# Zero writes to the row memory and the scatters in front of them, declared independent

## The chip, the cores and the metric

The kernel runs on one core of one Trainium2 chip. The metric is the device time of one execution in microseconds (us), as the median of several runs; the kernel before has a median of 2022.66 us over 3 runs (2016.06 to 2024.6).

## The reference

A causal seven-tap convolution over the sequence, per head with softmaxed weights, is followed by a mixture of eight experts, of which each token takes the best two.

```python
w = softmax(weight)                                  # 8 heads x 7 taps
out = np.einsum('hk,bskhg->bshg', w, x_unf)          # 28672 tokens x 192
noisy = x @ w_gate + log1p(exp(x @ w_noise)) * noise # 28672 x 8
top2 = the two best experts of a token, top2_w their softmax
for e in range(8):
    h = np.maximum(x[mask] @ w1[e], 0.0)             # 192 -> 1024
    out[mask] += top2_w[mask, k, None] * (h @ w2[e]) # 1024 -> 192
```

## The kernel before

The 28672 tokens go through in 28 **units** of 1024 (128 partitions by 8). A unit is convolved (VectorE, at first TensorE), scaled, and split into high and low 16-bit halves in one of two row buffers `rb` (lines 595 to 605; unit u takes buffer u % 2). Its gate values are computed from the transposed rows `xT` (eight transposing loads of the SP queue from line 636, then TensorE at line 651), and VectorE works out for each token its place in the lists of its two experts (`idx`, line 762). GpSimd (POOL) then writes the rows there: 16 indirect DMAs of 128 rows a unit, the **scatters** of line 783, into the DRAM tensor `xs`, the row memory, in which each expert has its region. The first ScalarE copy into `rb` for unit u (line 599) cannot start before the scatters of unit u - 2 have landed, since they read that buffer.

The experts work in 232 **blocks** (29 rounds by 8 experts, 256 rows each but for the first round). A block's rows come from `xs` by two transposing loads (lines 938 and 941) into one of three buffers `bT`; TensorE makes the first product into `ph` (line 858), ScalarE and VectorE turn it into `h` (lines 881, 885), TensorE makes the second product into `py` (line 895), ScalarE scales it into one of six buffers `y` (line 902), and POOL adds `y` into the output by an indirect DMA (line 907), two a block. The adds of a block wait until those of the block before have landed. A round's table of tokens and gates, `mt`, is loaded at line 803.

The lists are full up to a bound that the draw decides, so the last rows of each expert's fixed blocks may never be written. For them `zero_rows` (line 455) writes zeros: eight DMAs of 384 rows by 800 bytes on the SP queue, one for each expert, spawned when unit 6 comes to its gating (line 617). `lo_row` is 6912, the first row of that stretch in a region of 7296. `reach[u + 1]` is the highest row that the scatters of unit u can reach: at most 6144 up to unit 5, and 7168 or more from unit 6 on. The scatters from unit 6 on are made to wait for all zero writes (lines 791 to 793).

The order of the instructions on every engine is fixed at build time by a planner with estimated durations (class `Plan`); a queue does nothing out of turn. Waits are put in by the tile framework from what the instructions read and write. Since an indirect DMA may write anywhere in `xs`, the framework sees each scatter and each zero write as writes to the same memory and orders them, unless they are declared independent (`tc.declare_no_dep` with a group's name).

Of the kernel before, what the change touches and what calls it, by code (L numbers as in the profile page):

```python
# [9 lines left out]
F16 = mybir.dt.float16  # L10
# [8 lines left out]
P = 128  # L19
TU = 8  # L20
ROW = 400
# [111 lines left out]
def kernel(  # L133
# [11 lines left out]
    nc = tc.nc  # L145
# [51 lines left out]
    zero = const.tile([P, ROWF], F32, name="zero")  # L197
# [59 lines left out]
    init = []  # L257
    lo_row = max(0, min(cap - P, int(mean * U - 3.3 * sigma * math.sqrt(U)) // P * P))
    reach = [0]
# [8 lines left out]
    def mark(*key):  # L268
        return marks.setdefault(key, Mark())

    def done(*key, after=0.0):
        plan.mark(mark(*key), after)
# [164 lines left out]
    scat, zeroed = {}, []  # L437
# [17 lines left out]
    def zero_rows():  # L455
        nz = (cap - lo_row) // P
        for e in range(E):
            yield SP, 0.5
            init.append(nc.sync.dma_start(
                xs[e * REG + lo_row:e * REG + cap, :].rearrange("(p r) c -> p r c", p=P),  # L460
                zero.bitcast(F16)[:, None, :].to_broadcast([P, nz, ROW])))
        done("zero rows")

    def loads_first():
# [76 lines left out]
    def due(u):  # L541
        n, t = at_block
        return t + sum(EACH * rounds[i // E][1] / BIG for i in range(n, needed[min(u, U - 1)] * E))
# [64 lines left out]
    def gating():  # L608
        for u in range(U):
# [7 lines left out]
            if u == 6:  # L617
                plan.spawn(zero_rows())
# [144 lines left out]
            scat[u] = []  # L763
            done("routed", u)
            plan.spawn(scatters(u, rbf, idx), 0.3)

    def needs(a, b):
        tc.add_manual_dep(a.ins, b.ins.name, mybir.DependencyInfo(
            mybir.DependencyClass.Sync, mybir.DependencyReason.DATA), reason="data in DRAM")

    def apart():
        nc.gpsimd.nop()

    def scatters(u, rbf, idx):
        if u:
            yield mark("scattered", u - 1)
        if reach[u + 1] > lo_row:
            yield mark("zero rows")
        for i in range(2 * TU):
            t, k = i // 2, i % 2  # L780
            yield POOL, 1.4
            apart()
            s = nc.gpsimd.indirect_dma_start(  # L783
                out=xsf, out_offset=bass.IndirectOffsetOnAxis(ap=idx[:, k, t:t + 1], axis=0),
                in_=rbf[:, t, :], in_offset=None)
            for v in scat:
                tc.declare_no_dep(s.ins, group=f"scat{v}", reason="every routed row has its own place")
            tc.declare_no_dep(s.ins, group="loads", reason="rows behind those of the blocks done")
            scat[u].append(s)
            tc.add_to_no_dep_group(f"scat{u}", s.ins)  # L790
            if reach[u + 1] > lo_row:
                for z in init:
                    needs(s, z)
            slack = (due(u) - 45.0 - plan.now) / (2 * TU - i)
            if u > 1:
                yield plan.now + min(2.6, max(0.0, slack - 1.4))
        done("scattered", u, after=2.5)
# [364 lines left out]
```

## Time and profile before

| what | value |
|---|---|
| median of the runs | 2022.66 us |
| the profiled execution, its own time | 2030.29 us |
| its span | 2028.3 us |
| TensorE busy | 1946.0 us, 96% |
| VectorE, POOL, ScalarE busy | 1557.7, 1263.0, 804.2 us |
| mean granted TensorE clock | 0.986 of full speed |

The page's engine lines say who is busy; the views of waits and the timelines say for what the others wait. POOL's busy time leaves out about 0.3 us of issue ahead of each of its 904 indirect DMAs.

### The profile page before, as it was taken

What the parts mean: (1) busy time and instruction counts of PE and PEld (TensorE: products, weight loads), DVE (VectorE), ACT (ScalarE), POOL (GpSimd) and SP (SyncE); (2) the same over time, 40 slices, a digit from 0 to 9 for tenths busy, and PEclk for the clock granted to TensorE, in tenths of its full rate; (3) what the DMA queues carried; (4) which work ended last, traced back from release to release, by engine and by line L of the source; (5) the groups of instructions that cost most, each with busy time, mean ns of one, the idle gap of its engine ahead of it and who ended that gap; (6) DMA issues with size and microseconds to landing.
All of it is one profiled execution on the core that took longest, in us unless ns stands there. A gap on an engine that the chain in (4) does not pass through costs nothing. (4 is left out here: it accounts for less than half of the span.)

```text
span 2028.3 us, 52446 instructions
## 1 busy us (share of the span) xinstructions
PE 1946.0 (96%) x21703; PEld 1785.3 (88%) x21703; DVE 1557.7 (77%) x4042; ACT 804.2 (40%) x1173; POOL 1263.0 (62%) x915
## 2 busy tenths in 40 slices
PE   7779999999999999999999999999989999999997
PEld 7668899898999999989989888899989999999996
DVE  7799899898998989989888887788778865333332
ACT  4464444333444444334433333334333333333332
POOL 0566776577666767676666667666666666633333
PEclk9889999999999999999999999999999999999999
DMA  8845566877787767677766676667766765444442
GB/s 242 220 101 102 111 130 116 151 134 117 130 138 133 121 116 140 117 134 127 133 122 111 113 131 124 115 112 125 115 115 96 115 113 91 85 59 64 58 58 37
DMA packets 521882, 236.99 MB, mean 117 GB/s; under 512 B 401304, under 2 KB 508824, under 8 KB 521505
## 3 DMA queue, kind: packets, MB, share of 16 engines
q1 hardware_dynamic: 433824, 142.72, 34.2%
q0 software_dynamic: 87200, 90.80, 30.0%
q8 instruction: 171, 2.80, 0.6%
q14 instruction: 79, 0.65, 0.1%
q10 hardware_dynamic: 608, 0.02, 0.0%
HBM read 40.12 MB, written 115.38 MB: 77 GB/s over the span
## 5 line engine op out<-in xcount | busy, mean ns | idle before, releaser
L907 POOL DMA_INDIRECT out_dram<-y,ids x456 | 762.8, 1673 | 534.5 <-ACT y L902 160.7
L858 PE MATMUL ph<-bT,w1s 128*128 128x256 f16 (+2 forms) x9280 | 994.3, 271 | 15.9 <-DMA bT<-xs 7.7
L895 PE MATMUL py<-w2s,h 128*128 128x192 f16 x10944 | 986.2, 247 | 22.4 <-ACT y L902 22.3
L895 PEld LDWEIGHTS <-h 128*128 128x128 f16 x10944 | 910.3, 98 | 61.1 <-issue 53.5
L858 PEld LDWEIGHTS <-w1s 128*128 128x128 f16 (+1 forms) x9280 | 786.5, 97 | 131.5 <-issue 40.3
L885 DVE SCALAR_TENSOR_TENSOR h<-ph,h 128x1024 f16<-128x1024 f32 (+1 forms) x464 | 557.8, 1202 | 340.1 <-ACT h L881 336.7
L881 ACT ACTIVATE h<-ph 128x1024 f16<-128x1024 f32 (+1 forms) x464 | 468.2, 1009 | 593.9 <-PE ph L858 577.5
L783 POOL DMA_INDIRECT xs<-rb,idx x448 | 498.5, 1113 | 212.3 <-issue 133.0
L576 DVE SCALAR_TENSOR_TENSOR xc<-xt,wt,xc 128x192 f32<-128x192 f32 x1224 | 420.3, 409 | 2.1 <-DMA xt<-zero 2.1
L902 ACT ACTIVATE y<-py,ga 128x192 f32<-128x192 f32 x456 | 191.8, 421 | 487.7 <-PE py L895 483.1
L528 PE MATMUL ph<-xt,dg 128*128 128x192 f32 x280 | 50.4, 339 | 13.9 <-DMA xt<-in_x_dram 11.7
L603 DVE TENSOR_TENSOR rb<-xc,rb 128x1024 f16<-128x1024 f32 x28 | 34.2, 1220 | 37.8 <-ACT rb L599 34.9
L528 PEld LDWEIGHTS ph<-xt,dg 128*128 128x128 f32 x280 | 47.4, 198 | 14.3 <-DVE dg L508 11.7
L599 ACT ACTIVATE rb<-xc 128x1024 f16<-128x1024 f32 x28 | 29.5, 1055 | 65.2 <-DMA xs<-rb,idx 35.2
L574 DVE TENSOR_SCALAR xc<-xt,wt 128x192 f32<-128x192 f32 x204 | 53.9, 328 | 1.3 <-DMA xt<-in_x_dram 0.7
L589 DVE TENSOR_REDUCE am<-xc 128x8 f32<-128x1536 f32 x28 | 48.9, 1748 | 4.2 <-ACT xc L583 3.7
L593 DVE TENSOR_TENSOR xc<-xc,xs 128x1536 f32<-128x1536 f32 x28 | 49.0, 1751 | 0.0
L687 DVE SCALAR_TENSOR_TENSOR t<-t,t 128x64 f32<-128x64 f32 x168 | 37.8, 225 | 5.3
L497 ACT ACTIVATE xt<-xt 128x1152 f32<-128x1152 f32 x27 | 31.2, 1154 | 0.0
L733 DVE TENSOR_REDUCE sums<-M 128x72 f16<-128x576 f16 x23 | 26.7, 1160 | 0.0
L651 PE MATMUL misc<-gparts,xT 128*128 128x32 f16 (+1 forms) x752 | 23.3, 174 | 1.4 <-DMA xT<-rb 1.4
L651 PEld LDWEIGHTS <-xT 128*128 128x128 f16 x752 | 22.7, 96 | 1.9 <-DMA xT<-rb 1.5
(142 smaller groups left out, 613.9 us busy)
## 6 DMA issues: line engine op xcount, KB each, us to landing
out_dram<-zero SPq DMA_DIRECT2D x28, 768.0 KB
xt<-in_x_dram SPq DMA_DIRECT2D x27, 768.0 KB
bT<-xs SPq DMA_TRANSPOSE x464
out_dram<-y,ids POOLq DMA_INDIRECT x456
xs<-rb,idx POOLq DMA_INDIRECT x448
w2s<-in_moe_w_dram SPq DMA_DIRECT2D x16, 384.0 KB
w1s<-in_moe_w_dram SPq DMA_DIRECT2D x8, 512.0 KB
w1s<-in_moe_w_dram SPq DMA_DIRECT2D x16, 256.0 KB
```

The source lines that it names most:

```text
L528: nc.tensor.matmul(c[:, h - h0, :TU * G].rearrange("p (t g) -> p t g", g=G), diag[h, k], xts[u][:, k:k + TU, h * G:(h + 1) * G], start=(k ...
L574: V.tensor_scalar(dst, src, wt[:, h, k:k + 1], None, op0=OP.mult)
L576: V.scalar_tensor_tensor(dst, src, wt[:, h, k:k + 1], dst, op0=OP.mult, op1=OP.add)
L589: V.tensor_reduce(am, xc, axis=AX.X, op=OP.max, apply_absolute_value=True)
L593: V.tensor_tensor(xc, xc, xsc[:, :, None].to_broadcast([P, TU, D]), op=OP.mult)
L783: s = nc.gpsimd.indirect_dma_start(out=xsf, out_offset=bass.IndirectOffsetOnAxis(ap=idx[:, k, t:t + 1], axis=0), in_=rbf[:, t, :], in_offs ...
L858: nc.tensor.matmul(ph[:, f, :T], w, x, start=opens and f // 2 not in banks[:i], stop=closes and f // 2 not in banks[i + 1:], skip_group_ch ...
L881: nc.scalar.activation(h[:, 0, half * nf:(half + 1) * nf, :T], ph[:, :, :T], AF.Relu)
L885: V.scalar_tensor_tensor(h[:, 1, hs, :T], ph[:, :, :T], 0.0, h[:, 0, hs, :T], op0=OP.max, op1=OP.subtract)
L895: nc.tensor.matmul(py[:, half, :D], h[:, a, f, ts], w2_part(e, lo, f), start=(n == 0), stop=(n == 3 * FC - 1), skip_group_check=True)
L902: nc.scalar.activation(y, py, AF.Copy, scale=gate)
L907: a = nc.gpsimd.indirect_dma_start(out=out, out_offset=bass.IndirectOffsetOnAxis(ap=ids, axis=0), in_=y, in_offset=None, compute_op=OP.add)
```

## The change

The zero writes get the group name "zero rows", and are declared independent of the scatters of the units that are already recorded and whose rows end at or below `lo_row`. The scatters of such units that are recorded after a zero write are declared independent of the group. The waits of the scatters from unit 6 on, which do reach these rows, stay.

```diff
-            init.append(nc.sync.dma_start(
+            z = nc.sync.dma_start(
                 xs[e * REG + lo_row:e * REG + cap, :].rearrange("(p r) c -> p r c", p=P),
-                zero.bitcast(F16)[:, None, :].to_broadcast([P, nz, ROW])))
+                zero.bitcast(F16)[:, None, :].to_broadcast([P, nz, ROW]))
+            for v in scat:
+                if reach[v + 1] <= lo_row:
+                    tc.declare_no_dep(z.ins, group=f"scat{v}", reason="the unit's rows lie in front")
+            tc.add_to_no_dep_group("zero rows", z.ins)
+            init.append(z)
...
             if reach[u + 1] > lo_row:
                 for z in init:
                     needs(s, z)
+            else:
+                tc.declare_no_dep(s.ins, group="zero rows", reason="rows in front of these")
```

No instruction changes its place on any engine; only waits differ. On the SP queue, among the transposes of unit 6 (`xT`) and the loads of blocks (`bT`), the two single waits for POOL's DMAs shown here go, and a third ahead of the first zero write ten rows earlier. DMASW are the semaphores of POOL's DMAs, DMAHW those of the SP queue's. Before:

```order
L636 DMA_TRANSPOSE xT<-rb_189 128x3x128 [waits DMAHW7_49]
L459 DMA xs<-zero 384x1x400 [waits DMAHW0_49,DMASW2_49]
L459 DMA xs<-zero 384x1x400 [waits DMAHW1_49]
L459 DMA xs<-zero 384x1x400 [waits DMAHW2_49]
L938 DMA_TRANSPOSE bT<-xs 128x3x256 [waits DMAHW3_49,PE_49]
L941 DMA_TRANSPOSE bT<-xs 128x256 [waits DMAHW4_49]
L459 DMA xs<-zero 384x1x400 [waits DMAHW5_49,DMASW3_49]
```

And with the change:

```order
L641 DMA_TRANSPOSE xT<-rb_189 128x3x128 [waits DMAHW7_49]
L459 DMA xs<-zero 384x1x400 [waits DMAHW0_49]
L459 DMA xs<-zero 384x1x400 [waits DMAHW1_49]
L459 DMA xs<-zero 384x1x400 [waits DMAHW2_49]
L945 DMA_TRANSPOSE bT<-xs 128x3x256 [waits DMAHW3_49,PE_49]
L948 DMA_TRANSPOSE bT<-xs 128x256 [waits DMAHW4_49]
L459 DMA xs<-zero 384x1x400 [waits DMAHW5_49]
```

What moved: nothing but the waits DMASW2 and DMASW3.

On POOL, in the scatters of unit 5 (`rb_191`) between adds of expert blocks, three scatters wait for zero writes; two of them stand here. Before:

```order
L783 DMA xs<-rb_191,idx 287744x200 [waits DMAHW1_49,DMAHW2_49,DMAHW0_49,DMASW3_49]
L907 DMA out_dram<-y,ids 28928x192 [waits DMASW7_49,DMAHW7_49,DMASW1_49,Activation_49]
L907 DMA out_dram<-y,ids 28928x192 [waits DMASW5_49,Activation_49]
L783 DMA xs<-rb_191,idx 287744x200 [waits DMAHW6_49,DMAHW5_49,DMAHW7_49,DMAHW0_49,DMASW6_49]
L783 DMA xs<-rb_191,idx 287744x200
```

And with the change:

```order
L788 DMA xs<-rb_191,idx 287744x200 [waits DMASW3_49]
L914 DMA out_dram<-y,ids 28928x192 [waits DMASW7_49,DMAHW7_49,DMASW1_49,Activation_49]
L914 DMA out_dram<-y,ids 28928x192 [waits DMASW5_49,Activation_49]
L788 DMA xs<-rb_191,idx 287744x200 [waits DMASW6_49]
L788 DMA xs<-rb_191,idx 287744x200
```

What moved: the waits for the zero writes leave unit 5. They come back in one place, the first scatter of unit 6 (`rb_189`), eleven rows on, which before waited for VectorE's `idx` alone and now waits for it and for seven DMAHW semaphores; the load of a round's table `mt` behind the zero writes names two more DMASW semaphores.

## Rows read from the trace of the kernel before

**Rows 1.** The page's first lines: span; busy us, share, instructions by engine.

```profile
span 2028.3 us, 52446 instructions
PE 1946.0 (96%) x21703; PEld 1785.3 (88%) x21703; DVE 1557.7 (77%) x4042; ACT 804.2 (40%) x1173; POOL 1263.0 (62%) x915
```

**Rows 2.** Waits, 340 to 420 us, POOL and SP: us in total, times, longest.

```profile
POOL xs L783 <- DMA xs<-zero: 15.7, 3, 7.8
SPq L459 <- DMA xs<-rb,idx: 10.2, 3, 3.9
```

**Rows 3.** POOL's timeline: start, duration, instruction, [idle before, releaser].

```profile
343.16 2.02 POOL L907 DMA_INDIRECT out_dram<-y,ids  x1 [0.30 <-issue]
...
357.60 0.98 POOL L783 DMA_INDIRECT xs<-rb,idx  x1 [2.13 <-DMA xs<-zero]
...
378.87 1.00 POOL L783 DMA_INDIRECT xs<-rb,idx  x1 [7.80 <-DMA xs<-zero]
...
389.44 0.99 POOL L783 DMA_INDIRECT xs<-rb,idx  x1 [5.80 <-DMA xs<-zero]
...
458.60 1.98 POOL L907 DMA_INDIRECT out_dram<-y,ids  x1 [0.31 <-issue]
...
519.78 2.68 POOL L907 DMA_INDIRECT out_dram<-y,ids  x1 [0.30 <-issue]
526.50 1.56 POOL L907 DMA_INDIRECT out_dram<-y,ids  x1 [4.04 <-ACT y L902]
...
1044.69 1.59 POOL L907 DMA_INDIRECT out_dram<-y,ids  x1 [0.31 <-issue]
```

**Rows 4.** ScalarE's timeline: result copies `y` and row copies `rb`.

```profile
341.74 0.42 ACT L902 ACTIVATE y<-py,ga 128x192 f32<-128x192 f32 x1 [0.96 <-PE py L895]
...
402.44 1.06 ACT L599 ACTIVATE rb<-xc 128x1024 f16<-128x1024 f32 x1 [3.51 <-DMA xs<-rb,idx]
...
439.19 0.42 ACT L902 ACTIVATE y<-py,ga 128x192 f32<-128x192 f32 x1 [1.50 <-PE py L895]
...
465.86 1.06 ACT L599 ACTIVATE rb<-xc 128x1024 f16<-128x1024 f32 x1 [6.40 <-DMA bT<-xs]
...
1031.59 0.42 ACT L902 ACTIVATE y<-py,ga 128x192 f32<-128x192 f32 x1 [1.40 <-issue]
...
1052.14 1.06 ACT L599 ACTIVATE rb<-xc 128x1024 f16<-128x1024 f32 x1 [4.30 <-DMA xs<-rb,idx]
```

**Rows 5.** TensorE's timeline: the gaps of 340 to 480 us and normal rows.

```profile
373.15 0.24 PE L651 MATMUL misc<-gparts,xT 128*128 128x32 f16 x3 [1.37 <-DMA xT<-rb]
...
403.86 2.14 PE L895 MATMUL py<-w2s,h 128*128 128x192 f16 x24 [1.72 <-ACT y L902]
...
463.15 1.91 PE L858 MATMUL ph<-bT,w1s 128*128 128x256 f16 x16
468.70 3.39 PE L895 MATMUL py<-w2s,h 128*128 128x192 f16 x24 [3.65 <-ACT y L902]
471.89 2.36 PE L858 MATMUL ph<-bT,w1s 128*128 128x256 f16 x16
474.08 2.14 PE L895 MATMUL py<-w2s,h 128*128 128x192 f16 x24
```

**Rows 6.** TensorE's timeline, 480 to 1120 us: its three gaps there.

```profile
874.59 2.14 PE L895 MATMUL py<-w2s,h 128*128 128x192 f16 x24 [1.86 <-ACT y L902]
...
1055.42 0.39 PE L858 MATMUL ph<-bT,w1s 64*128 64x256 f16 x4 [2.02 <-DVE h L885]
...
1119.50 0.40 PE L858 MATMUL ph<-bT,w1s 64*128 64x256 f16 x4 [1.34 <-DVE h L885]
```

**Rows 7.** Stretches: us, then busy PE, PEld, DVE, ACT, POOL, PEclk, DMA share, GB/s.

```profile
380.00:400.00 20.00, 20.00 (x224) 18.22 (x223) 17.60 (x51) 8.38 (x12) 11.89 (x9) 1.00 0.87 187
460.00:480.00 20.00, 16.35 (x166) 14.29 (x163) 13.13 (x38) 6.61 (x9) 13.02 (x11) 0.91 0.78 137
1040.00:1060.00 20.00, 17.98 (x182) 15.82 (x180) 14.36 (x26) 8.08 (x11) 14.27 (x11) 0.91 0.68 143
```

## The prediction

> **What bounds the kernel now.** I read the page's engine lines first, then the waits around the zero writes, then three timelines side by side: POOL, ScalarE, TensorE. TensorE is busy for 1946.0 of 2028.3 us [rows 1], so the bound is TensorE, and an edit can only give back what lies in the other 82 us: gaps of TensorE, and time in which its clock was low. The waits that the change takes away stand on POOL, 15.7 us in three waits, and on the SP queue, 10.2 us in three [rows 2]. Neither engine is the bound, and TensorE had no gap at all while four of the zero writes were under way (20.00 of 20 us busy at 380 to 400 [rows 7]). So the question is how late POOL is afterwards, and who pays for it.
>
> That is read by pairing the n-th result copy `y` with the n-th add (456 of each). The 51st `y` starts at 341.74 and its add at 343.16: POOL is 1.0 us behind the end of the copy [rows 3, 4]. Then come the three waits of 2.13, 7.80 and 5.80 us [rows 3]. The 74th `y` starts at 439.19 and its add at 458.60, 19.0 us behind. The 218th, ten units later, is still 1044.69 - 1031.59 - 0.42 = 12.7 us behind [rows 3, 4]. POOL does not catch up, because it is full: each DMA costs its duration and 0.3 us of issue, and the first add of a block waits until the last add of the block before has landed, as from 519.78 to 526.50 [rows 3], 6.7 us, while a block comes every 8.4 us or faster (1946.0 us / 232 blocks).
>
> What POOL's lateness does to TensorE is in ScalarE's rows [rows 4]. The row copy for unit 7 at 402.44 waited 3.51 us for the scatters of unit 5 to release `rb`; that for unit 8 at 465.86 waited 6.40 us. (That row names a load of `bT`; the copy does not read it, and the last scatter of unit 6 had just been issued, so I take it for the same wait.) ScalarE works in order, so the next `y` stands behind the row copy, `py` is not emptied, and TensorE stops: 1.72 us at 403.86, 3.65 us at 468.70 [rows 5].
>
> **The change part by part.** No instruction is added, taken away or moved; six waits go, and one comes back later.
>
> The first three waits of SP. The transposes of unit 6 go out behind them, and TensorE waited 1.37 us for the last at 373.15 [rows 5]. The three waits are 10.2 us with a longest of 3.9 us [rows 2], so the first is at least 2.4 us, more than the gap, and the gap goes: **1.4 us**. What is late next is a load of `bT` between the two, whose buffer TensorE frees; that can cost a part of the lead, and only if it costs over 1 us does the gap stay in part.
>
> The three waits of POOL. Without them the scatters of unit 5 end up to 15.7 us earlier. What takes their place is the adds, which may not go ahead of their `y`. At the 51st add POOL is only 1.0 us behind, and the growth of the lag to the 74th is 18 us, about the 15.7 us of waits and 2 us beside; so almost the whole lead is real, and I take 14 to 15 us. The first row copy waited 3.51 us and the second 6.40 us, both far less than that, so both waits go, and with them the two gaps: 1.72 + 3.65 = **5.4 us** [rows 4, 5].
>
> The clock. After the 3.65 us gap the granted clock is 0.91 in the mean of 460 to 480 us [rows 7]: for a while TensorE is at the lower of its two levels. The two groups of rows behind the gap took 3.39 and 2.36 us where the same groups take 2.14 and 1.91 us beside it [rows 5]: 1.25 + 0.45 = **1.7 us**.
>
> So far 1.4 + 5.4 + 1.7 = 8.5 us, all between 360 and 480 us.
>
> The rest of the lead. At 470 us the kernel before has lost 3.65 + 1.7 us of TensorE's time to the stall, and POOL caught up by as much; the changed one keeps the remaining 15 - 8.5 = 6.5 us as a smaller lag. Later stalls of the same kind follow at 874.59 (1.86 us), 1055.42 (2.02 us) and 1119.50 (1.34 us) [rows 6]; in front of the second ScalarE's row copy waited 4.30 us [rows 4], less than 6.5. If the lag is that much smaller all along, the first two go, with the low clock behind the second (0.91 again at 1040 to 1060 us [rows 7], which I take at the same 1.7 us): 1.86 + 2.02 + 1.7 = **5.6 us**. The lead is then 15 - 14.1 = 0.9 us, and the stall at 1119.50 stays for the most part. A lead of POOL can be spent by TensorE once, so 15 us is also the ceiling.
>
> The waits that come back. The first scatter of unit 6 now names the zero writes, and the load of `mt` two more scatters. That scatter stands eleven of POOL's DMAs behind the last of the three waits, and eleven of the shortest take 11 x (0.98 + 0.30) = 14 us [rows 3], so the zero writes have landed by then: no cost. VectorE, which in the kernel before sits behind that `mt`, gets a few microseconds; I count none. Were the zero writes later than that, POOL would wait in unit 6 as it now does in unit 5.
>
> **Sum:** 1.4 + 5.4 + 1.7 + 5.6 = 14.1 us. Against the profiled execution, 2030.29 - 14.1 = 2016.2 us (2.0 us of it lie around the span). That execution is 7.6 us above the median of the runs shown, 2022.66; I subtract the same from the median: **2008.6 us**. The bounds are 3.1 us (the two first gaps alone) and 8.5 + 5.6 + 1.34 + 1.7 = 17.1 us, somewhat over the ceiling of 15 us.
>
> **The rivals.**
>
> *The lag forms again.* Between 343 and 458 us POOL also lost about 2 us more than the waits; if that goes on wherever scatters and adds share the engines, POOL is back at its 12.7 us before 870 us, and only the part up to 480 us is kept: 8.5 us, 2014.2 us. For it: the lag is nearly as large ten units later as it was behind the waits [rows 3, 4], so something may hold it there. Against it: nothing on POOL's side is seen that would make it later when it is less late; its waits are for landings and follow its own issues.
>
> *The waits only change their names.* The scatters of unit 5 may have had to wait for something else at these three places; one of the three also waits for its own earlier DMAs. Then only the SP part stays: about 1.4 to 3 us, 2020 us. Against it: the trace puts all 15.7 us down to the zero writes, by what came last [rows 2].
>
> *Slower: the zero writes crowd out the loads.* Eight writes of 384 rows by 800 bytes are 2.46 MB; the kernel before spreads them over some 30 us by the very waits that go. Put closer together, with the loads of blocks behind them on the SP queue, they could bring `bT` late. Two blocks are loaded ahead, some 16.8 us of TensorE's work. At the 187 GB/s of 380 to 400 us [rows 7] 2.46 MB take 13.2 us, which is covered; it decides from 16.8 us on, when they get less than 146 GB/s beside all else. At 80 GB/s they take 31 us, TensorE waits 14 us and loses 1.7 us to the clock, and the scatters land late as well, so that the gain is gone: 2022.66 + 15.7 = 2038 us. The row speaks against it: at a DMA share of 0.87 TensorE had no gap [rows 7]. The Trainium skill (DMA: Bandwidth & Descriptors, "Queues, rings and completion order") says that a DMA engine takes turns between the queues that have work for it, a packet at a time; so zero writes issued earlier would also slow POOL's scatters and adds, which speaks against this change. By its figure of about 27 GiB/s for each of 16 engines the 2.46 MB are an estimated 5.3 us of all engines, which by itself would not outlast the lead.
>
> **How the numbers follow.** The forecast, a gain of 10 to 17 us with 14.1 the likeliest: 0.54. The lag that forms again, 3 to 10 us: 0.32. Only names: 0.08. Slower: 0.06. A measurement of this kernel can tell about 0.5% from no change, 10.1 us. Faster by more than that is the forecast, 0.54, and of the second case a little that is over the line by the scatter of the runs (8.5 us from lowest to highest), 0.01: 0.55. Slower is the last case alone, 0.05, as a part of it ends within the line. The rest is the same: 0.40. The range goes from the ceiling with half the scatter of the runs, 2022.66 - 17.1 - 4.3 = 2001, to the end of the third case, 2022: that leaves out the slower case and the tails of the others.
>
> **What would show it.** POOL without a wait of a scatter for a zero write in unit 5, and the add of the 74th `y` less than 8 us behind it; no gap of TensorE at the last transposes of unit 6 and none behind the row copies of units 7 and 8; a granted clock of 1.00 there; at 870 and 1050 us the row copies without a wait for scatters. If the add lag is small at 440 us and back over 10 us at 860 us, the second case holds. If POOL's scatters wait 15 us for another DMA in the same places, the third. If TensorE waits for `bT` between 370 and 420 us, the last. The forecast is also wrong if runs without the profiler do not have these stalls at all: they are 7.6 us shorter, and I cannot see from which place.

## The result and the profile after

The changed kernel takes 2011.88 us in the median of 15 runs (2006.93 to 2025.02). The kernel before, timed beside it on the same chip, takes 2029.52 us in 15 runs (2016.06 to 2041.69), more than the 2022.66 us of the three runs shown ahead. The ratio is 0.9915, with a 95% interval of 0.9893 to 0.9937. (Ratios, here and below, are of undisturbed runs alone and need not equal the quotient of the medians.) The medians differ by 17.6 us, the two profiled executions by 19.1 us (2030.29 and 2011.19).

The page of the changed kernel begins so (compare [rows 1]):

```profile
span 2009.2 us, 52443 instructions
PE 1940.0 (97%) x21703; PEld 1781.4 (89%) x21703; DVE 1559.7 (78%) x4042; ACT 804.2 (40%) x1173; POOL 1260.8 (63%) x915
```

TensorE runs the same 21703 matmuls in 6.0 us less busy time, and the rest of the 19.1 us is idle time. The groups of instructions say which. First the two large groups of TensorE before (busy us, mean ns of one | idle us just before them, and what ended it), then the same after:

```profile
L858 PE MATMUL ph<-bT,w1s 128*128 128x256 f16 (+2 forms) x9280 | 994.3, 271 | 15.9 <-DMA bT<-xs 7.7 <-DVE h L885 5.3 <-DVE w1s L426 1.4
L895 PE MATMUL py<-w2s,h 128*128 128x192 f16 x10944 | 986.2, 247 | 22.4 <-ACT y L902 22.3
```

```profile
L865 PE MATMUL ph<-bT,w1s 128*128 128x256 f16 (+2 forms) x9280 | 992.9, 271 | 11.1 <-DMA bT<-xs 7.7 <-DVE w1s L426 1.8 <-ACT w1s L424 1.0
L902 PE MATMUL py<-w2s,h 128*128 128x192 f16 x10944 | 982.0, 247 | 12.7 <-ACT y L909 12.6
```

Waits of TensorE for a result copy `y` fall from 22.3 to 12.6 us, those for `h`, 5.3 us before, are no longer among the first three, and the busy times of the two groups fall by 1.4 and 4.2 us: stretches of lower granted clock that are gone (in the mean the granted clock is 0.986 before and 0.988 after). Together that is 4.8 + 9.7 + 1.4 + 4.2 = 20.1 us, about the whole difference. Waits for loads of `bT` are 7.7 us in both.

POOL's and SP's waits from 340 to 420 us (the same window as [rows 2], where the waits for zero writes and for scatters stood):

```profile
POOL xs L788 <- issue: 6.4, 21, 0.3
POOL out_dram L914 <- DMA out_dram<-y,ids: 5.9, 2, 3.7
```

```profile
SPq L945 <- PE ph L865: 20.6, 6, 5.4
```

No scatter waits for a zero write, and no zero write for a scatter. What the scatters have left is their own issue, 0.3 us each. The 74th and the 218th result copy and add, for which [rows 3, 4] give 19.0 and 12.7 us of lag (ScalarE's and POOL's timelines; start, duration, instruction, [idle before, releaser]):

```profile
436.87 0.42 ACT L909 ACTIVATE y<-py,ga 128x192 f32<-128x192 f32 x1 [1.50 <-PE py L902]
...
1023.45 0.42 ACT L909 ACTIVATE y<-py,ga 128x192 f32<-128x192 f32 x1 [1.40 <-PE py L902]
```

```profile
440.70 1.59 POOL L914 DMA_INDIRECT out_dram<-y,ids  x1 [0.30 <-issue]
...
1029.17 1.59 POOL L914 DMA_INDIRECT out_dram<-y,ids  x1 [0.30 <-issue]
```

The lag is now 440.70 - 436.87 - 0.42 = 3.4 us, and 5.3 us ten units later. So the row copies find `rb` free (ScalarE, units 7, 8 and 18; [rows 4] has waits of 3.51, 6.40 and 4.30 us at these places):

```profile
399.69 1.06 ACT L604 ACTIVATE rb<-xc 128x1024 f16<-128x1024 f32 x1 [1.06 <-DVE xc L598]
...
456.90 1.06 ACT L604 ACTIVATE rb<-xc 128x1024 f16<-128x1024 f32 x1
...
1039.81 1.06 ACT L604 ACTIVATE rb<-xc 128x1024 f16<-128x1024 f32 x1
```

The stretches of [rows 7] (us, then busy PE, PEld, DVE, ACT, POOL, granted clock, DMA share, GB/s):

```profile
380.00:400.00 20.00, 20.00 (x224) 18.25 (x223) 17.72 (x51) 8.37 (x13) 13.01 (x9) 1.00 0.73 146
460.00:480.00 20.00, 20.00 (x221) 18.64 (x220) 18.36 (x52) 7.22 (x10) 14.73 (x11) 1.00 0.93 153
1040.00:1060.00 20.00, 20.00 (x224) 18.24 (x222) 17.21 (x44) 9.47 (x13) 12.61 (x10) 1.00 0.81 140
```

TensorE is without a gap in all three, at its higher level. Its first gap behind 340 us is new, 1.51 us for a transpose; the next come only behind 1160 us (those of [rows 5, 6] stood at 373, 404, 469, 875, 1055 and 1120). The first and the largest but one of the new list:

```profile
487.11 0.24 PE L656 MATMUL misc<-gparts,xT 128*128 128x32 f16 x3 [1.51 <-DMA xT<-rb]
...
1235.53 3.57 PE L902 MATMUL py<-w2s,h 128*128 128x192 f16 x24 [2.79 <-ACT y L909]
```

Where the time was won follows from the start of the n-th `y` in both traces (the changed execution begins its blocks 1.2 us later; taken off): 8.6 us are won by the 81st, at 465 us; 7.3 at the 177th, behind the new gap; 14.7 by the 241st, at 1116 us; 20.3 by the 289th, at 1317 us; and 20.5 at the end.

### The profile page after: what moved, and what is told of

Same layout as the page of the kernel before. It is cut to its first block, busy times and chain, and to the rows that moved or that the text cites. A ratio compares the mean times of both kernels' runs of the same rounds, so it can differ in the third digit from the quotient of the medians.

```text
span 2009.2 us, 52443 instructions
## 1 busy us (share of the span) xinstructions
PE 1940.0 (97%) x21703; PEld 1781.4 (89%) x21703; DVE 1559.7 (78%) x4042; ACT 804.2 (40%) x1173; POOL 1260.8 (63%) x915
## 5 line engine op out<-in xcount | busy, mean ns | idle before, releaser
L902 PE MATMUL py<-w2s,h 128*128 128x192 f16 x10944 | 982.0, 247 | 12.7 <-ACT y L909 12.6
L533 PE MATMUL ph<-xt,dg 128*128 128x192 f32 x280 | 50.5, 340 | 14.9 <-DMA xt<-in_x_dram 11.6
L608 DVE TENSOR_TENSOR rb<-xc,rb 128x1024 f16<-128x1024 f32 x28 | 34.2, 1222 | 26.7 <-ACT rb L604 23.9
L604 ACT ACTIVATE rb<-xc 128x1024 f16<-128x1024 f32 x28 | 29.6, 1055 | 41.8 <-DMA xs<-rb,idx 21.5
L738 DVE TENSOR_REDUCE sums<-M 128x72 f16<-128x576 f16 x23 | 26.7, 1162 | 0.0
```

Of the source, the lines that this page charges most:

```text
L533: nc.tensor.matmul(c[:, h - h0, :TU * G].rearrange("p (t g) -> p t g", g=G), diag[h, k], xts[u][:, k:k + TU, h * G:(h + 1) * G], start=(k ...
L902: nc.tensor.matmul(py[:, half, :D], h[:, a, f, ts], w2_part(e, lo, f), start=(n == 0), stop=(n == 3 * FC - 1), skip_group_check=True)
```

## The experiments

My theory was: POOL's three waits make its queue late, and with it the scatters; `rb` is released late; ScalarE's row copy waits for it, the `y` behind the copy waits too, and TensorE stops with `py` full and then runs at the lower clock for a while. The rival worth testing was that the gain comes from elsewhere: from SP's queue, from the DMA engines' load, or from another timing that has nothing to do with the lag. Runs of one group are on one chip with the kernel before beside them; the groups are on different chips, so each is read by itself. A trace shows one execution of its kernel, and executions differ: that of the first experiment, 2027.71 us, is the longest of its seven runs, that of the third, 2020.82 us, the shortest of its twelve.

### First group: either half, the lag, and the copies (before: 2033.71 us)

**One half: POOL's scatters wait as before, SP's zero writes don't.**

```diff
             if reach[u + 1] > lo_row:
                 for z in init:
                     needs(s, z)
-            else:
-                tc.declare_no_dep(s.ins, group="zero rows", reason="rows in front of these")
```

> One half of the change: the zero writes no longer wait for the scatters in front, but the scatters still wait for the zero writes. Theory (POOL's lag makes ScalarE's row copies wait, and those stop TensorE): the zero writes go out earlier, so POOL's three waits shrink from 15.7 us to 4 to 10 us but stay; the add of the 74th y is 8 to 14 us behind; TensorE's gap at the last transposes of unit 6 is gone; gain 4 to 12 us against the kernel before. Rival (the waits on the SP queue were what cost): the whole gain, 15 us and more, with POOL still waiting.

Measured: 2015.36 us (2008.43 to 2027.71), ratio 0.9909 [0.9876, 0.9942]: as much as the whole change gained on its own chip (0.9915). Of POOL's 15.7 us this is left:

```profile
POOL xs L788 <- DMA xs<-zero: 1.2, 1, 1.2
```

I had expected POOL waits of 4 to 10 us to stay, a lag of 8 to 14 us and a gain of 4 to 12 us, and was wrong: issued without waits (the first, second and fifth at 350.57, 368.00 and 373.75 us, where the kernel before has 354.06, 373.32 and 381.29), the zero writes hold POOL up only for that 1.2 us, and the lag at the 74th `y` is 6.9 us.

**The other half: SP's zero writes wait as before, POOL's scatters don't.**

```diff
-            for v in scat:
-                if reach[v + 1] <= lo_row:
-                    tc.declare_no_dep(z.ins, group=f"scat{v}", reason="the unit's rows lie in front")
```

> The other half: the scatters of unit 5 no longer wait for the zero writes, but the zero writes still wait for the scatters in front. Theory (POOL's lag): POOL's 15.7 us of waits are gone, SP's stay at 5 to 10 us; the lag of the adds at the 74th y is under 8 us; the gaps of TensorE behind the row copies of units 7 and 8 and at 870 and 1050 us are gone; gain 13 to 19 us. Rival (SP's waits were what cost): gain under 4 us.

Measured: 2013.65 us (2006.95 to 2021.99), ratio 0.9902 [0.9866, 0.9938]: as much again. SP still waits, and a small gap at the transposes stays (SP's waits, TensorE's timeline):

```profile
SPq L459 <- DMA xs<-rb,idx: 7.1, 2, 3.7
```

```profile
370.93 0.24 PE L653 MATMUL misc<-gparts,xT 128*128 128x32 f16 x3 [0.88 <-DMA xT<-rb]
```

The gaps at 404, 469, 875 and 1055 us are gone, as expected. But this trace has others that I had not expected, 4.9 us in three gaps from 771 to 808 us and 6.35 us at 995 us; so has that of the first half. Those at 808 and 995 us stand behind row copies that waited 4.75 and 8.36 us for scatters; the other two are taken up below.

The halves do not add up: each gives all, as far as these ratios can tell. The two sets of waits were one loop. SP's zero writes waited for POOL's scatters, POOL's next scatters for those zero writes, and in between each queue held up what stood behind it. Breaking either side ends it; POOL's 74th add is 6.9 us behind with the one half and 7.3 with the other. Which of the two edits does it makes no difference that I can measure; the lag does.

**The change, with POOL made late by other means.** Idle instructions, which write a buffer that nothing reads, hold POOL up at three of unit 5's scatters where the kernel before waited.

```diff
+            if u == 5:
+                for _ in range({5: 4, 10: 14, 11: 10}.get(i, 0)):
+                    nc.gpsimd.iota(idle, pattern=[[1, 512]], base=0, channel_multiplier=0)
             apart()
             s = nc.gpsimd.indirect_dma_start(
```

> The changed kernel with 28 small index fills on POOL (an estimated 0.5 to 0.6 us each, from the 0.23 us of the fill of 128 columns and 0.12 us of that of 8 in the trace) before the 6th, 11th and 12th scatter of unit 5, where the kernel before waited for zero writes; no wait comes back. Theory (POOL's lag, whatever makes it): lag of 14 to 20 us at the 74th y, the gaps behind the row copies of units 7 and 8 come back, time within 6 us of the kernel before. Rival (the waits themselves, or the spread of the zero writes, cost): the time of the changed kernel, 15 us and more below the kernel before.

Measured: 2033.78 us (2020.82 to 2042.21), ratio 1.0004 [0.9982, 1.0026]: all of the gain is gone, with not one of the old waits back. Nor do the idle instructions slow another engine: VectorE's two main groups take 411 and 1220 ns an instruction from 355 to 400 us, 409 and 1220 in the change. The group of the idle instructions, then the row copy of unit 7 and TensorE behind it:

```profile
L790 POOL IOTA idle<- 128x512 int32 x28 | 16.8, 599 | 1.7
```

```profile
403.16 1.06 ACT L605 ACTIVATE rb<-xc 128x1024 f16<-128x1024 f32 x1 [6.68 <-DMA xs<-rb,idx]
```

```profile
404.58 4.00 PE L906 MATMUL py<-w2s,h 128*128 128x192 f16 x24 [4.89 <-ACT y L913]
```

This is the theory's chain, made by hand: POOL late by 16.8 us, the copy waits 6.68 us for the scatters, TensorE stands 4.89 us. Two details missed: the 74th add is 9.3 us behind, not 14 to 20, and unit 8's copy does not wait. The longer first stall, 4.89 us in place of 1.72, in which POOL catches up, explains some 3 of the 10 us by which the lag is smaller than before; the rest is open.

**The kernel before, with the row copies placed later.** The planner lets a copy into `rb` be placed when, by its estimate, the scatters that read the buffer are done plus 2.5 us. From unit 5 on this margin becomes 14 us. No wait is touched; the order behind unit 7 changes on all engines.

```diff
             if u >= NRB:
-                yield mark("scattered", u - NRB)
+                yield mark("released", u - NRB)
...
         done("scattered", u, after=2.5)
+        done("released", u, after=14.0 if u >= 5 else 2.5)
```

> The kernel before, with all its waits, but the planner is told that from unit 5 on the row buffers come free 14 us after the last scatter is issued instead of 2.5 us, so that ScalarE's row copies stand later in its order. Theory (the lag costs only through ScalarE's row copies): POOL's 15.7 us of waits and a lag over 10 us stay, but the row copies of units 7 and 8 wait less than 1 us and TensorE's gaps behind row copies are gone up to 1100 us; gain 8 to 20 us. Rival (the lag costs through the adds and the y buffers, or through something else of POOL): gain under 4 us.

Measured: 2011.25 us (2009.78 to 2019.19), ratio 0.9919 [0.9888, 0.995]. POOL is as late as ever, 21.3 us at the 74th add, with its old waits:

```profile
POOL xs L783 <- DMA xs<-zero: 14.7, 3, 7.1
```

The copies of units 7 and 8 still waited 1.78 and 6.97 us where I had expected less than 1, and TensorE 4.06 us behind the second; up to 820 us its waits for `y` are 13.2 us, against 5.4 before. The gain is made later, since behind 820 us this execution has no gap of TensorE for a `y` or `h` but the two of 0.51 us near its end, which the kernel before has too. So a good part of what the lag costs is paid where ScalarE's queue reaches a row copy before POOL is through. Since the order behind unit 7 changed on all engines, this run alone does not say how much; the third group has the copies' own rows.

But the theory that the lag costs *only* through the copies does not hold, and the rival in my expectation is half right. Where the lag is large, TensorE also stops with no row copy near (ScalarE, TensorE):

```profile
448.67 0.42 ACT L903 ACTIVATE y<-py,ga 128x192 f32<-128x192 f32 x1 [4.09 <-DMA out_dram<-y,ids]
```

```profile
449.14 2.14 PE L896 MATMUL py<-w2s,h 128*128 128x192 f16 x24 [1.35 <-ACT y L903]
```

This is the 77th `y`, and it waits for POOL's own DMA: with six buffers `y` it takes the buffer of the 71st, whose add started 5.98 us earlier and was 20.9 us behind its copy. Five such gaps are 5.6 us of TensorE's time in this execution (at 449, 603, 608, 645 and 705 us; the `y` of that at 608 names another releaser), against 7.6 us in three gaps behind row copies. The gaps at 771 and 784 us of the second experiment are of this kind, and two of the first and three of the third. In six traces 37 `y` copies wait over 2 us for an add, and each time the add six places ahead was 19 to 24 us late. The two traces of the first result have none: the lag of the kernel before passes 20 us at one add only, and the `y` that needs its buffer waits 1.18 us.

### Second group (before: 2053.8 us)

On this chip every kernel takes 1 to 2% longer, and behind 330 us TensorE shows 9 to 27 pauses a trace, of 0.15 to 1.8 us, that the trace puts down to issue. The change itself was not timed here.

**Half the idle work of the third experiment above** (2, 7 and 5 instructions):

> The changed kernel with 14 of the index fills on POOL (0.60 us each in the run with 28), so half of the lag is put back: 8.4 us. Theory with a threshold (lag costs only where a row copy comes before the scatters have landed): lag of 10 to 14 us at the 74th y, no gap of TensorE behind the row copies of units 7 and 8, 3 to 9 us above the changed kernel, ratio to the kernel before 0.993 to 0.997. Theory of a fixed share (all of POOL's lost time is paid for at once): 8.4 us above, 0.9955, with gaps at units 7 and 8. Rival (the lag does not matter): 0.991.

Measured: 2050.23 us (2040.42 to 2055.94), ratio 0.9969 [0.9943, 0.9994]. The ratio is in the first range, but the lag at the 74th `y`, 6.7 us, is not, and without the change beside it the run decides nothing; the third group repeats it.

**The change and the row copies later, with a margin of 10 us:**

> The changed kernel, and the planner told that from unit 5 on the row buffers come free 10 us after the last scatter is issued instead of 2.5 us. Theory (what is left of TensorE's gaps after 800 us is the same row copies): the row copies of units 20, 21, 22, 24 and 25 wait under 2 us each instead of 2.3 to 7.0 us, TensorE's gaps behind them go (some 9 us and the low clock behind two of them); gain 20 to 30 us against the kernel before. Rival (the later place costs as much in VectorE's and POOL's work as the gaps cost): the time of the changed kernel or worse.

Measured: 2031.49 us (2029.13 to 2041.18), ratio 0.9874 [0.9852, 0.9897]; the gain by medians is 22.3 us and the copies of units 20 to 25 wait for nothing, both as expected.

**The kernel before and the change, one execution each:**

> The kernel before on the chip of these runs, for its trace: three waits of POOL for zero writes of 13 to 18 us in all, a lag of 15 to 21 us at the 74th y, gaps of TensorE behind the row copies of units 7 and 8.

> The changed kernel on the same chip, for its trace: no wait of POOL for zero writes, a lag under 8 us at the 74th y, no gap of TensorE behind the row copies of units 7 and 8; whether the lag grows past 15 us near 770 us, as it did in the runs with one half of the change, with no cause of theirs there.

Measured: 2055.39 and 2059.05 us. As times these single executions say nothing, on a chip where those of the kernel before run from 2046 to 2070 us. As traces they say two things. POOL's waits for zero writes come back in the kernel before at 14.6 us and are absent in the change. But the kernel before, 13.4 us late at the 74th add where I had expected at least 15, has a gap of only 0.53 us at unit 7, whose copy waits for VectorE and not for scatters, and none at unit 8, and gaps of 3 to 6 us behind 900 us: where the lag is paid differs from one execution to the next. And the change, whose lag is 3.4 us at the 74th `y` and 6.5 at the 153rd, has late gaps too, 5.88 us at 1344 and 5.62 us at 1547 us.

### Third group: four kernels on one chip (before: 2027.0 us)

The change itself had not been timed beside the kernels of the first group, and on the second chip every kernel was slower; so the four that matter were timed together. The differences below are those of medians, and where the ratios say something else, that stands beside them.

> The changed kernel beside the three others on one chip. Theory: ratio to the kernel before 0.989 to 0.994; no wait of POOL for zero writes, a lag under 9 us at the 74th y, no gap of TensorE behind the row copies of units 7 and 8.

> The changed kernel with the row copies planned 10 us behind the scatters, again, beside the changed kernel on one chip. Theory (what is left of TensorE's gaps after 1100 us is row copies that wait): 5 to 12 us below the changed kernel, ratio to the kernel before 0.984 to 0.990. Rival (the two measures give back the same gaps): within 3 us of the changed kernel.

> The kernel before with its waits, and the row copies planned 10 us behind the scatters. Theory (lag costs where a row copy comes before its scatters have landed): POOL still waits 13 to 18 us for zero writes and lags 15 us and more at the 74th y, more than the 10 us allow, so units 7 and 8 still pay; later units do not; gain 8 to 18 us, 4 to 12 us less than with the change as well.

> The changed kernel with 14 index fills on POOL (8.4 us), again, on the chip of the changed kernel itself. Theory with a threshold: no gap behind the row copy of unit 8, 3 to 9 us above the changed kernel. Theory of a fixed share: 8.4 us above, with gaps behind units 7 and 8. Rival (the lag does not matter): as the changed kernel.

| kernel | median us (runs) | ratio to before [95%] | add lag at the 74th `y` |
|---|---|---|---|
| the change | 2011.07 (12) | 0.9951 [0.9921, 0.9981] | 5.2 us |
| the change, copies later (10 us) | 1998.41 (6) | 0.989 [0.9842, 0.9938] | 3.1 us |
| before, copies later (10 us) | 2016.77 (12) | 0.9953 [0.9923, 0.9982] | 13.4 us |
| the change, half the idle work | 2022.43 (12) | 0.9984 [0.995, 1.0017] | 11.5 us |

*The change alone* has no wait for zero writes, a lag of 5.2 us and no gap behind units 7 and 8, as expected. Its ratio, 0.9951, is just outside the 0.989 to 0.994 that I had expected: by medians the gain is 15.9 us here, by the ratio 9.9 us, with an interval of 4 to 16.

The group of second products of TensorE, in this order (idle time behind the second bar):

```profile
L902 PE MATMUL py<-w2s,h 128*128 128x192 f16 x10944 | 982.2, 247 | 12.1 <-ACT y L909 12.0
```

```profile
L903 PE MATMUL py<-w2s,h 128*128 128x192 f16 x10944 | 980.1, 246 | 3.6 <-ACT y L910 3.6
```

```profile
L896 PE MATMUL py<-w2s,h 128*128 128x192 f16 x10944 | 983.4, 247 | 21.1 <-ACT y L903 21.0
```

```profile
L906 PE MATMUL py<-w2s,h 128*128 128x192 f16 x10944 | 981.8, 247 | 21.1 <-ACT y L913 21.1
```

The four waits for `y`, 12.0, 3.6, 21.0 and 21.1 us, stand in the order of the four times, though the last two, all but equal, belong to times 5.7 us apart.

*Half the lag.* The question was whether half of the lag is free, because the copies of units 7 and 8 have some slack, or costs half. The place says free, the sum says no (ScalarE, units 7, 8, 10 and 14 of that kernel):

```profile
399.93 1.06 ACT L605 ACTIVATE rb<-xc 128x1024 f16<-128x1024 f32 x1 [0.59 <-DVE xc L599]
...
457.62 1.06 ACT L605 ACTIVATE rb<-xc 128x1024 f16<-128x1024 f32 x1
...
574.82 1.06 ACT L605 ACTIVATE rb<-xc 128x1024 f16<-128x1024 f32 x1 [2.91 <-DMA xs<-rb,idx]
...
815.79 1.06 ACT L605 ACTIVATE rb<-xc 128x1024 f16<-128x1024 f32 x1 [5.42 <-DMA xs<-rb,idx]
```

```profile
L790 POOL IOTA idle<- 128x512 int32 x14 | 9.0, 643 | 0.8
```

No copy waits for scatters at 400 or 458 us, but one does at 575 and another at 816, and `y` waits for adds in between (ScalarE, TensorE):

```profile
792.57 0.42 ACT L913 ACTIVATE y<-py,ga 128x192 f32<-128x192 f32 x1 [4.80 <-DMA out_dram<-y,ids]
```

```profile
793.04 2.14 PE L906 MATMUL py<-w2s,h 128*128 128x192 f16 x24 [2.75 <-ACT y L913]
```

So the lag acts as a debt: it is carried for 200 to 400 us and then paid. POOL is later than in the change alone by 6.3 us at the 74th `y`, 9.8 at the 100th and 8.4 at the 153rd, and no longer so at the 177th (8.5 us late against 11.5). By 820 us TensorE has stood 11.7 us in five gaps where the change alone has none over 0.3 us: 5.4 us behind the copies of units 10 and 14, and 6.3 us for `y` buffers that POOL's adds still hold, at 642, 777 and 793 us. The 9.0 us of idle work cost 11.4 us against the change by medians, above the 3 to 9 us of the one expectation, but 6.7 us by the two ratios, and the intervals of these overlap (0.995 to 1.0017 and 0.9921 to 0.9981). That the half costs something is clear; whether in full is not.

*The copies later.* With the change it gives 12.7 us more, a little over the 5 to 12 us that I expected. Behind 330 us and up to the last 20 us its trace has one gap of TensorE of over 0.3 us, 1.87 us at 1046. The copy of unit 25, at which the change alone waited for the scatters and TensorE then stood 4.58 us, is free (ScalarE in the change alone, then with the copies later):

```profile
1500.78 1.06 ACT L604 ACTIVATE rb<-xc 128x1024 f16<-128x1024 f32 x1 [6.37 <-DMA xs<-rb,idx]
```

```profile
1496.23 1.06 ACT L604 ACTIVATE rb<-xc 128x1024 f16<-128x1024 f32 x1
```

Without the change it stays 18 us above that (13 by the ratios; I had expected 4 to 12), because POOL's lag still stops TensorE in both ways. The first stop is at unit 7 (ScalarE, TensorE):

```profile
404.11 1.06 ACT L599 ACTIVATE rb<-xc 128x1024 f16<-128x1024 f32 x1 [5.00 <-DMA xs<-rb,idx]
```

```profile
405.53 3.45 PE L896 MATMUL py<-w2s,h 128*128 128x192 f16 x24 [3.21 <-ACT y L903]
```

I had expected units 7 and 8 to pay and later ones not to. Unit 8 does not; units 10, 14 and 15 do, and the four copies together cost TensorE 10.8 us. A further 6.6 us in five gaps from 608 to 797 us are `y` copies that wait for adds, which a later row copy does not cure.

So the two measures are different cures of one illness: one takes the debt away, the other asks for payment later, at the copies alone. Together they make the fastest version measured, 1998.41 us, and in the second group 0.9874 of the kernel before. In the third group its interval still overlaps a little with that of the change alone.

Not tried: a third buffer `rb`, against the copies' waits, or more buffers `y`, against the waits for adds; either would have put one of the two ways to the test without moving anything.

## Why the prediction was right, and where it was not

The forecast was 2008.6 us, a gain of 14.1; measured were 2011.88 us and 17.6. Both are in the range, and the likeliest case is the one that came. Its steps:

- **The bound and the chain: right.** TensorE has the same work, POOL and SP are never the bound, and the gain is in TensorE's gaps. The third experiment made the chain by hand. The second way, by `y` buffers that the adds still hold, is not in the prediction; it has no share in the two traces compared here, and appears in the experiments where POOL is some 20 us late.
- **SP's three waits, 1.4 us: right in the trace of the change,** whose gap at the transposes is gone. With SP's waits kept, 0.88 us of it stays.
- **The lead of POOL, 14 to 15 us: right.** The 74th add is at 3.4 instead of 19.0 us, a lead of 15.6.
- **SP's part, units 7 and 8 and the clock, together 8.5 us by 480 us: right,** 8.6 us. That the row naming a load of `bT` at 465.86 us [rows 4] was a wait for scatters is supported, since the wait goes with the lag, but the trace never names it so.
- **The rest of the lead, 5.6 us at 870 and 1050 us: right in size,** 14.7 us by 1116 us against 14.1, and both gaps are gone. A new gap, 1.51 us for a transpose at 487, was not in the sum, and the stall at 1119.50 went too, which I had said would stay; the two offset each other, so the close agreement is partly luck. Nor is the lag at 1045 us simply what the waits left, as I read it: in the kernel before it falls from 19.0 us to 8.5 at the 120th `y` and rises again to 13.9 at the 153rd, and in the third group the change, without the waits, is 12.1 us late at the 218th, where the kernel before had 12.7 in the trace of [rows 3, 4].
- **"A lead of POOL can be spent by TensorE once, so 15 us is also the ceiling": wrong.** This is the step that failed. From 1116 to 1317 us a further 5.6 us were won. By 1200 us POOL has caught up in the kernel before too (the 257th add is 2.7 us behind, and 7.4 in the change; the 289th 2.9 and 3.0), so there the lead is spent and, by my ceiling, nothing more could come. But units 20 to 22 stop TensorE anew, with a lag of a few microseconds, since their copies stand close behind the scatters; and they stop it less in the change, 3.9 us in all against 7.3: the copy of unit 22 waits 5.34 us before and 2.34 us after (ScalarE's timelines; the first row names a load of the noise, which the copy does not read, while the last scatter was issued 4.3 us ahead of it):

```profile
1314.76 1.06 ACT L599 ACTIVATE rb<-xc 128x1024 f16<-128x1024 f32 x1 [5.34 <-DMA nzt<-in_moe_noise_dram]
```

```profile
1297.15 1.06 ACT L604 ACTIVATE rb<-xc 128x1024 f16<-128x1024 f32 x1 [2.34 <-DMA xs<-rb,idx]
```

  What decides how much is paid there I did not settle. (That more than 15 us were won is so in this pair of traces, 20.5 us; the medians, 17.6 and in the third group 15.9 us, are hardly above the ceiling.) In the third group the same kernel has other late gaps, of 3.84 us at 1303 and 4.58 us at 1502.
- **The base: off by 6.9 us,** since the kernel before has a median of 2029.52 us over 15 runs. Taking the profiled execution's distance from three runs off the median cost more than the whole rest of the error. The gain was forecast 3.5 us too small and the base 6.9 us too low, and the two hide each other in part: that the sum came within 3.3 us is partly luck.

The rivals. *The waits only change their names* fell: no other DMA holds the scatters of unit 5. *Slower, by zero writes that crowd out the loads*, fell: the writes are closer together, the last issued at 376.20 us (384.20 before). Seven of the eight are issued from 368 to 376 us now, and there TensorE has no gap although the DMA engines are full (a share of 1.01), with waits for `bT` of 7.7 us in both kernels over the whole span (before, then after; columns as in [rows 7]):

```profile
360.00:380.00 20.00, 18.63 (x222) 17.51 (x223) 18.55 (x49) 6.86 (x11) 9.79 (x8) 1.00 0.81 140
```

```profile
360.00:380.00 20.00, 20.00 (x242) 18.46 (x240) 19.61 (x53) 7.63 (x12) 16.14 (x13) 1.00 1.01 197
```

The rule of the Trainium skill (DMA: Bandwidth & Descriptors, "Queues, rings and completion order") that a DMA engine takes turns between queues, a packet at a time, would have slowed POOL's DMAs. In POOL's own time no such price stands out: from 350 to 400 us the mean scatter takes 1135 ns before and 1197 after, but 1060 and 1049 ns in the second group's pair of traces; what it did to landings these rows do not show. *The lag forms again* is half right, and deserved its 0.32. In the profiled execution of the change it rises from 3.4 us to 9.8 at the 153rd `y`, but stays below the 13.9 of before. In the third group's execution of the same kernel it is 5.2 us at the 74th `y`, 14.4 at the 153rd and 14.9 at the 225th; that is the case as I had put it, and it is paid at unit 19 (ScalarE, TensorE):

```profile
1106.52 1.06 ACT L604 ACTIVATE rb<-xc 128x1024 f16<-128x1024 f32 x1 [8.86 <-DMA xs<-rb,idx]
```

```profile
1109.80 0.61 PE L865 MATMUL ph<-bT,w1s 64*128 64x256 f16 x4 [6.59 <-DVE h L892]
```

Both halves of the change show 22 us at the 153rd. So something besides the zero writes makes POOL late between 600 and 800 us, in some executions. POOL's idle time ahead of adds from 680 to 780 us does not explain it: 26.7 us in the second experiment, 25.5 in the kernel before and 25.8 in the change. The cause is open. It may be part of why the ratio of the third group lies nearer to 1 than the first result.

## What to carry to other kernels

Pair the n-th piece of work of a producer with the n-th of its consumer queue, and follow the lag: POOL's busy share, 62 and 63%, was the same with and without the trouble. Two DMA queues that wait for each other over one DRAM tensor make a loop; break either side, and do not expect the halves to add up. A late helper queue is a debt that an in-order engine pays wherever it reaches a shared buffer too early. List every buffer that the queue holds (here `rb` and `y`) before you say where it is paid. Where the lag can't be removed, give the waiting instruction a later place, and best do both.

## What the runs showed of the hardware

A queue of DMAs of 1 to 2 us with 0.3 us of issue each and a landing between blocks (6.7 us from one block's last add to the next block's first [rows 3]) recovers slowly: idle work of 9.0 us on POOL from 356 us on was still 8.4 us of extra lag at the 153rd add, some 400 us later. With six buffers `y`, a copy waited over 2 us for an add only where that add was 19 us late and more. And executions of one program differ in which copies wait, not only in how long: the copies of units 7 and 8 waited 3.51 and 6.40 us in one trace of the kernel before, and not for scatters at all in another, on another chip. One of the three chips of the groups made every kernel 1 to 2% slower, with many short pauses of TensorE that no releaser explains.
